# Moving the last 64 keys' value products to another place in an attention visit

## The chip, the core and the metric

The kernel runs on one core of one Trainium2 chip. The metric is the device time of one execution in microseconds (us), smaller being better. Several runs of the kernel are timed and their median is given. One further execution is recorded by the hardware profiler, and every line of a profile in this document comes from such an execution.

## What is computed

The reference normalises the rows of q and k, does attention, lays the heads side by side, and sends the result through a two-layer block whose activation is h - tanh(h):

```python
batch, n_heads, seq, head_dim = (8, 12, 448, 64)
q_n, k_n = (rmsnorm(q, g_q), rmsnorm(k, g_k))
scores = scale * np.matmul(q_n, k_n.transpose(0, 1, 3, 2))
scores = scores - np.max(scores, axis=-1, keepdims=True)
attn = np.exp(scores)
attn = attn / (np.sum(attn, axis=-1, keepdims=True) + 1e-09)
attn_out = np.matmul(attn, v)
x = attn_out.transpose(0, 2, 1, 3).reshape(B * S, H * D)     # 3584 x 768
h = x @ w_in                                                 # w_in 768 x 2048
g = h - np.tanh(h)
return g @ w_out                                             # w_out 2048 x 768
```

All of it is in float32.

## The kernel before

**Steps.** There are 48 steps s, one for each of the 8 batches and 6 pairs of heads. The 448 keys of a head are three blocks of 128 keys and a last block of 64. Scores lie with the keys on the partitions. For a step, `scores(s, c)` (L492) makes one wave of score matmuls: block c = 0, 1 or 2 of both heads, each head into a bank of PSUM of its own, then one exp per head on ScalarE (L512). For c = 3, written `KF`, both halves of the 448 queries are put under one another, so that the wave has 224 columns and not 448. The results are the tiles `p` (blocks 0 and 1), `p_full` (block 2) and `p_last` (the last 64 keys).

**Value products.** `half_values(s, c, av, first)` (L560) gives the value matmuls of block c in two groups: group 0 takes keys 0 to 63 of the block and adds into the bank `av[0]`, group 1 takes keys 64 to 127 and adds into `av[1]`. `last_values(s, av)` (L547) does the last 64 keys: four matmuls of 224 columns into `av[0]`, then four into `av[1]`. All these matmuls use a piece of the TensorE array of 64 rows and 32 columns, so that eight of them fill the array: two row halves by four column groups. A wave in this document is eight matmuls of the program that use the eight pieces; each is float32 and runs as two passes, so the trace shows 16 MATMUL records for a wave, in two rounds of eight.

**Banks.** From step 12 on the scores share three banks in turn (list `sc`, here called A, B and C), and the two `av` banks are fixed. Each `scores` call takes two banks. With the bank order of one visit written as A, B, C: the wave for the last keys takes A and B, block 0 takes C and A, block 1 takes B and C, block 2 takes A and B. A score matmul into a bank waits until the exp of the scores that were there before is done.

**A visit.** From step `FOLDED` = 13 on, the attention of a step is done by `visit(s, av)` (L579), 35 times in all; 34 of these have a next step, and for these the order of matmuls on TensorE is:

1. the scores of the next step's last keys (`scores(s + 1, KF)`, called in `slot`, L1010), into A and B;
2. `wave(*half_values(s, 2, av, True))`: the values of block 2, both groups, which start the sums in `av`;
3. `last_values(s, av)` (L582);
4. for c = 0 and then c = 1: a wave of head 0's scores of step s + 1 with group 1's values, and a wave of group 0's values with head 1's scores. The exp of each head is put on ScalarE's queue after its wave (L588, L590);
5. `divide(s, av)` (L594): ScalarE copies `av[0]` to `xT` (L670), VectorE adds `av[1]` (L671) and multiplies with the reciprocals of the sums of the weights (L675);
6. `scores(s + 1, 2)` (L596): the last wave of scores, heads alternating, into A and B, and its two exps.

**Between visits.** The two-layer block of the previous batch runs as a generator, `mlp()`. Calls of `run(ns)` in `slot` take matmuls from it, worth a given time by a fixed price per matmul, and put them on TensorE between visits (L733: 128 x 128 arrays of weights, 224 moving columns). Its products follow a Strassen-like scheme of seven products per set, in the order 1, 5, 6, 2, 3, 7, 4, with three banks of PSUM (`mm`) in turn; VectorE and ScalarE empty those banks (L787 for product 1, L789 for product 5, L791 for product 6, L795 and L796 for product 7, L799 for product 3, L803 for product 4). Weights are brought in by DMA to a ring of six places, issued from SyncE five products ahead. The order on each engine is written out by hand: each engine takes its instructions in the order in which the program issues them (`manual_schedule`), and semaphores keep the data right. After a visit `slot` issues the loads for later steps and, mixed with calls of `run`, the VectorE work for the sums and norms of the next steps (L537, L538, L458 to L462, L545, L640, L642, L470).

Of the kernel before, what the change touches and what calls it, by code (L numbers as in the profile page):

```python
# [137 lines left out]
def bounded_path(tc, ctx, q, k, v, moe_w_in, moe_w_out, out, g_col, ident, ones, half_ones, neg_half, early):  # L138
# [353 lines left out]
    def scores(s, c, apart=False):  # L492

        rr, kT, qT = turned[s]
        n = S if c < KF else HS
        name, bufs = ("p", 2) if c < 2 else ("p_full", 1) if c < KF else ("p_last", 2)
        if c == 1:
            p = probs[s, 1] = probs[s, 0]
        else:
            p = probs[s, c] = pp.tile([P, 2, 2 if c < 2 else 1, n], F32, name=name, bufs=bufs)  # L500
        tiles = [sc_bank() for _ in range(2)]

        def score(h, i):
            at, first = (i * BL, 0) if c < KF else (i * BL % KR, i * BL // KR * n)
            r = slice(h * D, (h + 1) * D)
            nc.tensor.matmul(  # L506
                tiles[h][i * BL : (i + 1) * BL, :n], lhsT=kT[r, c * P + at : c * P + at + BL],
                rhs=qT[r, first : first + n], start=True, stop=True,
            )

        def exp(h):
            nc.scalar.activation(  # L512
                p[:, h, c if c < 2 else 0, :], tiles[h][:, :n], AF.Exp,
                scale=1.0 if rr is None else rr[:, 0, 2 * c + h : 2 * c + h + 1],
            )

        if apart:
            return [(lambda i, h=h: score(h, i), lambda h=h: exp(h)) for h in range(2)]
        for i in range(P // BL):
            for h in range(2):  # L520
                score(h, i)
        for h in range(2):
            exp(h)
# [23 lines left out]
    def last_values(s, av):  # L547

        v_nat, p = loaded["v", s], probs[s, KF]
        for n in range(2):  # L550
            keys, at = slice(n * KR, (n + 1) * KR), n * HS if s >= FOLDED else 0
            for m in range(2):
                for h in range(2):
                    r = (2 * m + h) * BL
                    nc.tensor.matmul(  # L555
                        av[n][r : r + BL, at : at + HS], lhsT=v_nat[keys, h, KF, m * BL : (m + 1) * BL],
                        rhs=p[keys, h, 0], start=(s < FOLDED), stop=False, skip_group_check=(s >= FOLDED),
                    )

    def half_values(s, c, av, first):  # L560

        v_nat, p = loaded["v", s], full(s)[c]

        def value(g, i):
            m, h = i // 2, i % 2
            keys = slice(g * D, (g + 1) * D)
            nc.tensor.matmul(  # L567
                av[g][i * BL : (i + 1) * BL, :S], lhsT=v_nat[keys, h, c, m * BL : (m + 1) * BL],
                rhs=p[keys, h], start=first, stop=True, skip_group_check=not first,
            )  # L570

        return [lambda i, g=g: value(g, i) for g in range(2)]

    def wave(*work):
        for i in range(P // BL):
            for fn in work:
                fn(i)

    def visit(s, av):  # L579

        wave(*half_values(s, 2, av, True))
        last_values(s, av)  # L582
        for c in range(2):
            v0, v1 = half_values(s, c, av, False)
            if has(s + 1):
                (s0, exp0), (s1, exp1) = scores(s + 1, c, True)
                wave(s0, v1)
                exp0()  # L588
                wave(v0, s1)
                exp1()  # L590
            else:
                wave(v0, v1)
        del loaded["v", s]
        divide(s, av)  # L594
        if has(s + 1):
            scores(s + 1, 2)  # L596
# [68 lines left out]
    def divide(s, av):  # L665
        b, hp = steps[s]
        rs = whole.pop(s)
        x = xT[b, hp] = xp.tile([P, S], F32, name="xT")
        if s >= FOLDED:
            nc.scalar.copy(out=x, in_=av[0][:, :S])  # L670
            nc.vector.tensor_tensor(out=x, in0=x, in1=av[1][:, :S], op=ALU.add)  # L671
        for m in range(2):
            rows = slice(m * D, (m + 1) * D)
            if s >= FOLDED:
                nc.vector.tensor_tensor(out=x[rows], in0=x[rows], in1=rs, op=ALU.mult)  # L675
                continue
            for n in range(2):
                nc.vector.tensor_tensor(
                    out=x[rows, n * HS : (n + 1) * HS], in0=av[n][rows, :HS], in1=rs[n * D : (n + 1) * D],
                    op=ALU.mult,  # L680
                )
        for c in range(NCH):
            del probs[s, c]
        if hp < HC:
            return
        c = hp - HC
        if c == 0:
            tt[b] = tp.tile([P, 3, HC, HS], F32, name="tt", bufs=1)
        eng = nc.vector if b == 0 and c == HC - 1 else nc.gpsimd
        x11, x12, x21, x22 = (xT[b, r][:, n : n + HS] for r in (c, hp) for n in (0, HS))  # L690
        t1, t2, t4 = (tt[b][:, i, c] for i in range(3))
        eng.tensor_tensor(out=t1, in0=x12, in1=x11, op=ALU.subtract)
        eng.tensor_tensor(out=t2, in0=x22, in1=t1, op=ALU.subtract)  # L693
        eng.tensor_tensor(out=x12, in0=x22, in1=x12, op=ALU.subtract)
        eng.tensor_tensor(out=t4, in0=x21, in1=t2, op=ALU.subtract)
# [244 lines left out]
    def has(s):  # L940
        return 0 <= s < NS
# [63 lines left out]
    def slot(s):  # L1005
# [5 lines left out]
        if s < FOLDED:  # L1011
            last_values(s, av)
            totals(s, sc_bank())
            divide(s, values(s, av))
            for c in range(KF):
                scores(s + 1, c)
        else:
            visit(s, av)
# [405 lines left out]
```

## Time and profile before

| | |
|---|---|
| median of 3 runs | 1404.11 us (1401.81 to 1405.44) |
| profiled execution, its own time | 1404.34 us |
| span of the profiled execution (first to last instruction) | 1402.5 us |
| mean granted TensorE clock | 0.992 |
| first and last visit begin (first value matmul of block 2) | 317.76 and 1243.75 us |
| HBM traffic | 214.50 MB read, 33.42 MB written |

Engines are named PE (TensorE's matmuls), PEld (TensorE's weight loads), ACT (ScalarE), DVE (VectorE), POOL (GpSimd) and SP (SyncE). A group's line gives the source line, the engine, the operation, the tiles as out<-in, the shape, the number of instructions, the busy time, the mean duration of one in ns, and the idle time of the engine just ahead of the group with what ended it. A timeline line gives the start in us from the span's start, the duration, and the same names; instructions of one form that follow each other are merged in it, with their number after the x. Matmuls overlap: a MATMUL record of 536 ns in a wave doesn't mean that TensorE is taken for 536 ns, so the distance between the starts of rounds is what counts.

### The profile page before, as it was taken

The numbers are of one execution on the slowest core, as the hardware profiler recorded it, in microseconds if no ns is written. First come the engines' busy times: TensorE is split into PE (matmuls) and PEld (weight loads), VectorE is DVE, ScalarE is ACT, GpSimd is POOL, SyncE is SP. The second block draws the span as 40 slices with busy tenths as digits, with TensorE's granted clock in tenths as the row PEclk, the third lists the DMA queues.
The fourth block names the chain that finished last, engine by engine and source line by source line (L and its number), as shares of the span: only waits on it lengthen the run. The fifth ranks groups of instructions, "written<-read, shape, count | busy, mean of one in ns | idle before, by whom it ended". The sixth has DMA issues, their size and how long they took to land.

```text
span 1402.5 us, 29929 instructions
## 1 busy us (share of the span) xinstructions
PE 1367.2 (97%) x11864; PEld 1135.0 (81%) x11864; DVE 939.3 (67%) x1530; ACT 506.6 (36%) x1153; POOL 556.4 (40%) x348
## 2 busy tenths in 40 slices
PE   6999899999999999999999999999999999999997
PEld 2458664478888888888889988988988998899997
DVE  3999888866756688567867668656885678632311
ACT  5866554234422433233332333224333243301100
POOL 4665555223532246225544246422462254411310
PEclk9999999999999999999999999999999999999999
DMA  7769788864556656666666666666666666366563
GB/s 174 178 187 252 241 253 212 223 188 153 172 150 179 175 167 172 173 152 200 173 153 173 188 159 180 181 158 175 168 165 175 164 183 186 109 188 179 191 193 91
DMA packets 355273, 250.01 MB, mean 178 GB/s; under 512 B 266484, under 2 KB 297396, under 8 KB 355124
## 3 DMA queue, kind: packets, MB, share of 16 engines
q1 hardware_dynamic: 355120, 248.00, 64.7%
q8 instruction: 96, 1.57, 0.5%
q14 instruction: 53, 0.43, 0.1%
q10 hardware_dynamic: 4, 0.00, 0.0%
HBM read 214.50 MB, written 33.42 MB: 177 GB/s over the span
## 4 chain that ended last, share of the span: by engine, by line
PE 87%; DVE 5%; DMA 3%; ACT 2%; SPq 2%; issue 1%; POOL 0%; DVEq 0%; ACTq 0%
PE mm L733 64%; PE sc L506 9%; PE sc L567 6%; PE mm L898 4%; PE sc L555 1%; PE sc L605 1%; DMA w_raw<-in_moe_w_out_dram 1%; DMA gT<-in_moe_w_in_dram 1%; DMA q_nat<-in_q_dram 1%; ACT p L512 1%; SPq L118 1%; PE mm L605 1%; DMA w_f<-w_out 0%; DVE rs L631 0%; DVE w_out L82 0%
## 5 line engine op out<-in xcount | busy, mean ns | idle before, releaser
L733 PE MATMUL mm<-xT,w_f 128*128 128x224 f32 x1392 | 278.2, 354 | 2.3 <-DVE s L789 2.3
L733 PEld LDWEIGHTS mm<-xT,w_f 128*128 128x128 f32 x1392 | 261.3, 190 | 15.9 <-issue 10.2
L733 PEld LDWEIGHTS mm<-gT,w_f 128*128 128x128 f32 x1344 | 252.8, 190 | 13.2 <-issue 13.2
L733 PE MATMUL mm<-gT,w_f 128*128 128x224 f32 x1344 | 263.0, 354 | 0.0
L506 PE MATMUL sc<-qT,kT 64*32 64x448 f32 (+1 forms) x3072 | 219.3, 507 | 11.7 <-ACT p_last L512 7.8
L463 POOL TENSOR_TENSOR rr_mine<-rr_mine,neg_half 128x28 f32<-128x28 f32 x30 | 145.1, 4837 | 205.5 <-DVE rr_mine L462 205.5
L733 PE MATMUL mm<-tt,w_f 128*128 128x224 f32 x1044 | 208.9, 353 | 0.0
L733 PEld LDWEIGHTS mm<-tt,w_f 128*128 128x128 f32 x1044 | 196.6, 190 | 4.8 <-issue 4.4
L733 PE MATMUL mm<-tg,w_f 128*128 128x224 f32 x1008 | 197.7, 352 | 0.0
L770 POOL TENSOR_TENSOR gT<-s,th 128x448 f32<-128x448 f32 x96 | 119.1, 1250 | 189.4 <-ACT th L769 184.5
L733 PEld LDWEIGHTS mm<-tg,w_f 128*128 128x128 f32 x1008 | 190.6, 190 | 0.0
L506 PEld LDWEIGHTS sc<-qT,kT 64*32 64x32 f32 x3072 | 75.3, 106 | 87.7 <-issue 52.9
L671 DVE TENSOR_TENSOR xT<-xT,sc 128x448 f32<-128x448 f32 x35 | 21.7, 621 | 175.5 <-ACT xT L670 146.9
L693 POOL TENSOR_TENSOR tt<-xT,tt 128x224 f32<-128x224 f32 x23 | 31.4, 1367 | 243.6 <-DVE xT L675 222.0
L650 ACT COPY sum_g<-sum 32x14 f32<-32x14 f32 x280 | 56.2, 201 | 183.7 <-DVE sum L642 178.0
L567 PE MATMUL sc<-p,v_nat 64*32 64x448 f32 x1120 | 110.5, 536 | 0.0
L769 ACT ACTIVATE th<-s 128x448 f32<-128x448 f32 x96 | 55.2, 575 | 116.4 <-DVE s L795 57.2
L512 ACT ACTIVATE p<-sc 128x448 f32<-128x448 f32 x120 | 65.3, 544 | 58.0 <-PE sc L506 34.5
L135 POOL TENSOR_TENSOR rr<-rr,neg_half 112x8 f32<-112x8 f32 (+1 forms) x36 | 59.6, 1678 | 61.8 <-DVE rr L134 37.8
L898 PE MATMUL mm<-gT,w_out 128*128 128x448 f32 x192 | 75.5, 548 | 0.2 <-POOL w_out L90 0.2
L898 PEld LDWEIGHTS mm<-gT,w_out 128*128 128x128 f32 x192 | 36.1, 192 | 38.5 <-issue 36.4
L567 PEld LDWEIGHTS sc<-p,v_nat 64*32 64x32 f32 x1120 | 42.0, 107 | 30.6 <-issue 30.6
(151 smaller groups left out, 1853.7 us busy)
## 6 DMA issues: line engine op xcount, KB each, us to landing
w_f<-w_in SPq DMA_DIRECT2D x196, 384.0 KB, 3.3
w_f<-w_out SPq DMA_DIRECT2D x147, 512.0 KB, 4.0
w_raw<-in_moe_w_out_dram SPq DMA_DIRECT2D x16, 768.0 KB, 5.4
out_dram<-th SPq DMA_DIRECT2D x192, 56.0 KB, 1.9
w_in<-w_out SPq DMA_DIRECT2D x21, 384.0 KB, 6.5
qk_nat<-in_q_dram SPq DMA_DIRECT2D x120, 56.0 KB, 2.4
qk_nat<-in_k_dram SPq DMA_DIRECT2D x120, 56.0 KB, 2.4
gT<-in_moe_w_in_dram SPq DMA_DIRECT2D x32, 192.0 KB, 4.2
```

The costliest lines, as they stand in the source:

```text
L135: nc.gpsimd.tensor_tensor(out=r, in0=r, in1=neg_half[:rows], op=ALU.pow)
L463: nc.gpsimd.tensor_tensor(out=mine, in0=mine, in1=neg_half[:, :1].to_broadcast([P, 2 * NJ]), op=ALU.pow)
L506: nc.tensor.matmul(tiles[h][i * BL : (i + 1) * BL, :n], lhsT=kT[r, c * P + at : c * P + at + BL], rhs=qT[r, first : first + n], start=True ...
L512: nc.scalar.activation(p[:, h, c if c < 2 else 0, :], tiles[h][:, :n], AF.Exp, scale=1.0 if rr is None else rr[:, 0, 2 * c + h : 2 * c + h ...
L567: nc.tensor.matmul(av[g][i * BL : (i + 1) * BL, :S], lhsT=v_nat[keys, h, c, m * BL : (m + 1) * BL], rhs=p[keys, h], start=first, stop=True ...
L605: nc.tensor.matmul(av[n][r : r + BL, :HS], lhsT=v_nat[:, h, c, m * BL : (m + 1) * BL], rhs=p[c][:, h, n * HS : (n + 1) * HS], start=False, ...
L650: nc.scalar.copy(out=acc[h * BL : (h + 1) * BL, g], in_=part[g * BL : (g + 1) * BL, h * NJ : (h + 1) * NJ])
L693: eng.tensor_tensor(out=t2, in0=x22, in1=t1, op=ALU.subtract)
L733: nc.tensor.matmul(bank[:, f * HS : (f + 1) * HS], lhsT=w[:, c * width + f, :], rhs=moving[p](c), start=(first and f == 0 and c == 0), sto ...
L769: nc.scalar.activation(th, h, AF.Tanh, bias=0.0, scale=1.0)
L770: eng.tensor_tensor(out=g[:, rows, cols], in0=h, in1=th, op=ALU.subtract)
L898: nc.tensor.matmul(bank[:, :S], lhsT=w_out_row(f, n // HC)[:, n % HC * P : (n % HC + 1) * P], rhs=g[:, f, :], start=(f == 0), stop=(f == C ...
```

## The change

In `visit` the call of `last_values` is taken from its place behind the values of block 2 and put behind the two rounds of the loop over c. It thus stands ahead of `divide` and of the last wave of scores. Nothing else is touched: the matmuls, their operands and their number stay.

```diff
     def visit(s, av):
 
         wave(*half_values(s, 2, av, True))
-        last_values(s, av)
         for c in range(2):
             v0, v1 = half_values(s, c, av, False)
             if has(s + 1):
...
             else:
                 wave(v0, v1)
+        last_values(s, av)
         del loaded["v", s]
         divide(s, av)
         if has(s + 1):
```

On TensorE the eight matmuls of `last_values` move past the 32 matmuls of the loop. On ScalarE the order is the same, and the copy to `xT` (L670), which had no wait for TensorE of its own, has one. On VectorE, GpSimd and SyncE the order of instructions is the same.

## The prediction

> **What bounds the kernel now.** I read the page's busy times first, then its chain of the work that ended last, then the waits, and then the timelines of the visits.
>
> ```profile
> PE 1367.2 (97%) x11864; PEld 1135.0 (81%) x11864; DVE 939.3 (67%) x1530; ACT 506.6 (36%) x1153; POOL 556.4 (40%) x348
> ...
> PE 87%; DVE 5%; DMA 3%; ACT 2%; SPq 2%; issue 1%; POOL 0%; DVEq 0%; ACTq 0%
> ```
>
> TensorE sets the time: it is 97% busy, and 87% of the chain lies on it. But a busy figure hides short stops, because overlapping matmuls cover them. They show in the distances between starts. So I took one visit, the one that begins at 835.87 us, and read the starts on TensorE round by round (a round is eight matmuls, one for each piece of the array). First the rounds around the moved work, with the matmuls of the old place at L555:
>
> ```profile
> 836.24 0.58 PE L567 MATMUL sc<-p_full,v_nat 64*32 64x448 f32 x8
> 836.62 0.58 PE L555 MATMUL sc<-p_last,v_nat 64*32 64x224 f32 x16
> ```
>
> A round of 448 columns takes 0.375 us (836.24 to 836.62). The moved work is two rounds of 224 columns and takes 0.38 us, since block 0's first round starts at 837.00. From there eight rounds follow at 0.375 us each, 837.00 to 840.00, without a stop. Then comes the last wave of scores. Its weight loads, and beside them ScalarE:
>
> ```profile
> 839.63 0.11 PEld L506 LDWEIGHTS sc<-qT,kT 64*32 64x32 f32 x1 [0.22 <-ACT p L512]
> 840.00 0.34 PEld L506 LDWEIGHTS sc<-qT,kT 64*32 64x32 f32 x15 [0.27 <-issue]
> ```
> ```profile
> 838.84 0.55 ACT L512 ACTIVATE p<-sc 128x448 f32<-128x448 f32 x1 [0.22 <-PE sc L506]
> 839.57 0.54 ACT L512 ACTIVATE p<-sc 128x448 f32<-128x448 f32 x1 [0.19 <-PE sc L567]
> 840.34 0.54 ACT L512 ACTIVATE p<-sc 128x448 f32<-128x448 f32 x1 [0.23 <-PE sc L506]
> 840.78 0.53 ACT L670 COPY xT<-sc 128x448 f32<-128x448 f32 x1
> ```
>
> The wave's first matmul (head 0, bank A) starts at 840.00; in a narrower window of the timeline it is alone there, and the other seven start from 840.17 on. The second one (head 1) goes to bank B, whose scores of block 1, head 0, are read by the exp that ends at 839.57 + 0.54 = 840.11. So the whole wave loses 0.17 us to that exp. Afterwards the layer's first matmul (L733) starts at 841.08, which is 0.91 us behind the delayed start: two rounds and the run-out of the small pieces.
>
> The same reading in all 34 visits with a next step gives the same picture: the second matmul starts 0.14 to 0.33 us behind the first, and the sum is 6.3 us (mean 0.185).
>
> **A second place** where TensorE stops is between visits, once per batch, five times in the stretch of visits:
>
> ```profile
> 856.19 1.02 PE L733 MATMUL mm<-xT,w_f 128*128 128x224 f32 x4 [0.46 <-DVE s L789]
> ```
>
> The distance to the matmul before it is 0.63 us too long; the other four (at 530, 693, 1019 and 1182 us) are 0.60, 0.62, 0.55 and 0.72. VectorE comes late to empty a bank of the layer. The chain, read back from there, runs on VectorE alone, without a wait for TensorE, to the end of the visit:
>
> ```profile
> 840.89 0.43 ACT xT L670
> ...
> 841.34 0.63 DVE xT L671
> ...
> 855.52 0.62 DVE s L789
> ```
>
> So an earlier copy to xT moves that late step too.
>
> **What the Trainium skill says.** "TensorEngine Tiling (Array Packing)", Key Properties: tiles run independently, and a change of tiling mode drains the array. The trace agrees: eight matmuls of a round start within 0.05 us, and 841.08 is 0.16 us behind the end of two full rounds from 840.17 (the run-out). The moved matmuls have the tiling of both their old and their new neighbours, so no drain is added. "TensorE: Matmul & The Clock Gate", Part 3, The mechanism: matmuls start in program order, only weight loads are pulled ahead. The trace agrees: one waiting matmul held the six behind it in its round. "PSUM — Partial Sum Buffer", Engine vs sequencer instructions: ScalarE's queue is strictly first in, first out; so the copy's new wait could hold the exps behind it.
>
> **The change, part by part.** Times are within the visit above.
>
> 1. Removed at the old place: 0.375 us of matmuls between block 2's values and block 0's wave. All eight rounds start 0.375 us earlier, and so do the four exps that follow them: they end at 838.24, 839.01, 839.74 and 840.51.
> 2. New exposure of these rounds: head 1's scores of block 0 need bank A, head 0's of block 1 need bank B. The exps of p_last that free A and B begin at 836.21 and end at 836.57 and 836.81. The matmuls come at 837.37 and 838.12, their weight loads one round earlier. Left are 0.8 and 1.3 us to the matmul. In all visits those exps are within 0.1 us of this. Cost nothing; if ScalarE came 0.8 us later, this cover would be gone.
> 3. Added at the new place: two rounds of 224 columns, 0.375 us, from 839.63 to 840.00. TensorE has the same work ahead of the last wave of scores as before, which can again start at 840.00. Each float32 matmul is unchanged.
> 4. The stall: bank B is free at 839.74 plus the 0.06 us that lie between the exp's end and the start seen before, 839.80. The moved work covers this. In the worst visit (0.33 us) the release comes 0.05 us ahead of the wave. Gain 0.17 us here; over 34 visits 6.3 us. The last visit has no scores: nothing.
>    The unknown is how fast weights follow behind the short rounds: before, the eight loads behind L555 took from 836.81 to 836.96 and just fitted. With a wait among them they may end late by 0 to 0.1 us; I take 0, and keep 34 x 0.1 = 3.4 us for the range.
> 5. The new wait on ScalarE: the copy to xT waits for the moved matmuls. The last exp began 0.67 us behind the start of the last matmuls that it reads, of which 0.375 is streaming, so the tail is 0.29 us. The moved matmuls start their second pass at 839.82: 839.87 + 0.19 + 0.29 = 840.35 at the latest. ScalarE itself is free for the copy at 840.78 - 0.375 = 840.41. So the wait is covered by the exp, narrowly. Behind the copy are queued only the two exps of p_full, which need the last wave of scores (done about 841.0 either way).
> 6. VectorE's step L671 begins 0.375 us earlier, TensorE's layer work 0.17 us earlier. The five late emptyings (L789) sit at the end of an unbroken VectorE chain, so they come 0.375 us earlier while TensorE arrives 0.17 us earlier: each stop shrinks by 0.2 us, 1.0 us in all. Bounds: 0 (another step in the chain starts to wait) and 3.1 us (all five go).
> 7. DMA issues, GpSimd and SyncE: nothing is moved in their order. Loads of weights go by TensorE's progress; no matmul of L733 in the visits' stretch is shown waiting for a DMA.
>
> Sum: -6.3 - 1.0 = -7.3 us. Against the profiled execution's own 1404.34 us (span 1402.5 and 1.8 around it) that is 1397.0; it lies 0.2 us above the median of 1404.11, so for a median I say **1396.8 us**. TensorE bounds what follows to the end, with the layers of the last batches, so I expect what is saved in the visits to arrive there whole.
>
> **Rivals.**
>
> A. The forecast: 1396.8, with a spread of 1394.5 (all five stops go as well) to 1399.5.
>
> B. Half the gain: the stall is replaced by late weight loads, 0.1 us per visit, and VectorE's gain doesn't arrive: 1404.1 - 6.3 + 3.4 = 1401.2. For it: loads behind L555 were the slowest of the visit. Against: they fitted.
>
> C. Nothing arrives: TensorE comes 0.17 us earlier and waits for something between visits (a weight tile, a bank): 1404. For it: DMA is busy 60 to 70% in this stretch. Against: the five stops above are all that TensorE shows there, and VectorE gets more time, not less.
>
> D. Slower. The moved work no longer overlaps itself: in its new place the four matmuls on the upper row half and the four on the lower might run one group behind the other, as they are issued (n = 0, then n = 1), behind a round that mixes values and scores. Then it takes 0.75 us, 0.375 more than now, against the 0.185 gained: 34 x 0.19 = 6.5 us, 1410.6. It decides from 0.185 us of lost overlap on. Against: at the old place all 16 records lie in two rounds behind a full round, and the banks of the two halves differ from each other in both places.
>
> That the change doesn't do what it says is excluded: the order of instructions on TensorE shows the eight matmuls in the new place in all 35 visits.
>
> **How the numbers follow.** A 0.78, B 0.08, C 0.08, D 0.06. A change of 0.3% (4.2 us, about what a measurement of this kernel can tell from none) puts the border at 1399.9. A falls below it but for a few hundredths, B just above, C within, D above. Faster 0.79, same 0.15, slower 0.06. The range runs from 1394.5 to 1401.5: it takes in A and B, and leaves out C and D (0.14) and A's edges.
>
> **What would show it.** In the changed profile: block 0's first round 0.75 us behind block 2's values; the moved matmuls 3.75 us behind them in two rounds; the last wave of scores with its eight first-pass matmuls in one round, no wait for ScalarE; L733 at 5.05 us behind the visit's start, not 5.19 to 5.38; L671 about 0.37 us earlier; the five L789 stops at 0.35 to 0.5 us. Wrong would be: moved matmuls that span more than 0.4 us, a stop at banks A or B inside the loop, or new waits of L733.

## The result and the profile after

| | before | changed |
|---|---|---|
| median of 6 runs | 1404.12 us (1401.81 to 1405.44) | 1394.97 us (1393.06 to 1397.86) |
| profiled execution, its own time | 1404.34 us | 1397.86 us |
| span | 1402.5 us | 1396.1 us |
| first visit begins | 317.76 us | 319.21 us |
| from the first visit to the last | 925.99 us | 917.76 us |

The ratio of changed to before is 0.9939 (95% interval 0.9929 to 0.9949; the quotient of the two medians, 0.9935, lies inside it), so the change makes the kernel faster by 0.5 to 0.7%. The profiled execution of the changed kernel is its slowest of the six; its first visit begins 1.45 us later than in the profile of before, in a stretch that the change doesn't touch. The stretch from the first visit to the last (34 visits and what lies between them) is therefore the better yardstick: 8.23 us less.

The page looks as before:

```profile
PE 1360.6 (97%) x11864; PEld 1133.3 (81%) x11864; DVE 940.3 (67%) x1530; ACT 507.9 (36%) x1153; POOL 555.4 (40%) x348
...
PE 87%; DVE 5%; DMA 3%; ACT 2%; SPq 1%; issue 1%; POOL 0%; DVEq 0%; ACTq 0%
```

TensorE has lost 6.6 us of busy time with the same 11864 matmuls: a stop between overlapping matmuls counts as busy here, so what was saved shows there, while the idle time (span less busy time) is 35.3 us before and 35.5 us after. What happened is seen in the visit that answers to the one of the prediction, here from 832.78 us on. First the end of TensorE's visit in the timeline, then the weight loads of the same stretch:

```profile
836.54 0.58 PE L555 MATMUL sc<-p_last,v_nat 64*32 64x224 f32 x16
836.92 0.96 PE L506 MATMUL sc<-qT,kT 64*32 64x448 f32 x16
837.81 0.65 PE L733 MATMUL mm<-xT,w_f 128*128 128x224 f32 x2
```
```profile
836.54 0.15 PEld L555 LDWEIGHTS sc<-p_last,v_nat 64*32 64x32 f32 x8 [0.22 <-issue]
836.73 0.34 PEld L506 LDWEIGHTS sc<-qT,kT 64*32 64x32 f32 x16
837.80 0.30 PEld L733 LDWEIGHTS mm<-xT,w_f 128*128 128x128 f32 x2 [0.73 <-issue]
```

The moved matmuls take 0.38 us in their new place (836.54 to 836.92), as in the old one. The 16 records of the last wave stand in one line now, without the odd first one; the second matmul starts 0.007 us behind the first in all 34 visits. Its loads begin at 836.73, ahead of the matmuls at 836.92. Before, 14 of the 16 loads came together with the late matmuls. L733 starts at 5.03 us from the visit's start (mean of 34), before at 5.24.

ScalarE in the same visit, and then the stop once per batch:

```profile
836.11 0.54 ACT L512 ACTIVATE p<-sc 128x448 f32<-128x448 f32 x1 [0.19 <-PE sc L567]
836.90 0.54 ACT L512 ACTIVATE p<-sc 128x448 f32<-128x448 f32 x1 [0.25 <-PE sc L506]
837.35 0.53 ACT L670 COPY xT<-sc 128x448 f32<-128x448 f32 x1
```
```profile
852.74 1.02 PE L733 MATMUL mm<-xT,w_f 128*128 128x224 f32 x4 [0.29 <-DVE s L789]
```

The exp that frees bank B ends at 836.65, 0.27 us ahead of the last wave; in the tightest of the 34 visits it is 0.12 us. The copy to xT follows the last exp at the same distance as before, both 0.38 us earlier in the visit. The five stops at L789, measured as the excess of the distance between starts over the usual 0.187 us, are 0.40 to 0.46 us, 2.20 us in all, where they were 3.12.

### The profile page after: what moved, and what is told of

It is laid out like the page before. It is cut to its first block, busy times and chain, and to the rows that moved or that the text cites. A ratio compares the mean times of both kernels' runs of the same rounds, so it can differ in the third digit from the quotient of the medians.

```text
span 1396.1 us, 29929 instructions
## 1 busy us (share of the span) xinstructions
PE 1360.6 (97%) x11864; PEld 1133.3 (81%) x11864; DVE 940.3 (67%) x1530; ACT 507.9 (36%) x1153; POOL 555.4 (40%) x348
## 4 chain that ended last, share of the span: by engine, by line
PE 87%; DVE 5%; DMA 3%; ACT 2%; SPq 1%; issue 1%; POOL 0%; DVEq 0%; ACTq 0%
PE mm L733 65%; PE sc L506 9%; PE sc L567 6%; PE mm L898 4%; PE sc L555 1%; DMA q_nat<-in_q_dram 1%; PE sc L605 1%; DMA w_raw<-in_moe_w_out_dram 1%; DMA w_f<-w_out 1%; DMA w_raw<-in_moe_w_in_dram 1%; DVE w_out L82 1%; PE mm L605 1%; DVE w_out L78 0%; DVE rs L631 0%; ACT p L512 0%
## 5 line engine op out<-in xcount | busy, mean ns | idle before, releaser
L733 PE MATMUL mm<-xT,w_f 128*128 128x224 f32 x1392 | 278.2, 354 | 1.4 <-DVE s L789 1.4
L733 PEld LDWEIGHTS mm<-xT,w_f 128*128 128x128 f32 x1392 | 261.3, 190 | 15.0 <-issue 10.2
L733 PEld LDWEIGHTS mm<-gT,w_f 128*128 128x128 f32 x1344 | 252.8, 190 | 12.8 <-issue 12.8
L733 PE MATMUL mm<-gT,w_f 128*128 128x224 f32 x1344 | 263.0, 354 | 0.0
L733 PE MATMUL mm<-tt,w_f 128*128 128x224 f32 x1044 | 208.7, 353 | 0.0
L733 PEld LDWEIGHTS mm<-tt,w_f 128*128 128x128 f32 x1044 | 197.0, 190 | 4.4 <-issue 4.4
L733 PE MATMUL mm<-tg,w_f 128*128 128x224 f32 x1008 | 197.7, 353 | 0.0
L733 PEld LDWEIGHTS mm<-tg,w_f 128*128 128x128 f32 x1008 | 190.6, 190 | 0.0
L506 PEld LDWEIGHTS sc<-qT,kT 64*32 64x32 f32 x3072 | 72.3, 107 | 84.3 <-issue 58.8
L671 DVE TENSOR_TENSOR xT<-xT,sc 128x448 f32<-128x448 f32 x35 | 21.7, 621 | 163.3 <-PE sc L506 118.5
L512 ACT ACTIVATE p<-sc 128x448 f32<-128x448 f32 x120 | 65.2, 543 | 46.8 <-PE sc L506 34.5
```

Of the source, the lines that this page charges most:

```text
L506: nc.tensor.matmul(tiles[h][i * BL : (i + 1) * BL, :n], lhsT=kT[r, c * P + at : c * P + at + BL], rhs=qT[r, first : first + n], start=True ...
L512: nc.scalar.activation(p[:, h, c if c < 2 else 0, :], tiles[h][:, :n], AF.Exp, scale=1.0 if rr is None else rr[:, 0, 2 * c + h : 2 * c + h ...
L733: nc.tensor.matmul(bank[:, f * HS : (f + 1) * HS], lhsT=w[:, c * width + f, :], rhs=moving[p](c), start=(first and f == 0 and c == 0), sto ...
```

## The experiments

Theory 1 is that of the prediction: the last wave of scores waits for the exp that empties bank B, and the moved work covers that wait; beside this, an earlier copy to xT pulls VectorE's chain forward and shrinks the L789 stops. The rivals were that the old place of the matmuls was the costly one, that only VectorE's earlier start counts, or that the order counts whatever waits. All times "from the visit's start" are counted from the first value matmul of block 2; they and the delays are means over 34 visits, and the stops are sums, all from one profile per kernel.

| kernel | L733 | delay of the last wave's second matmul | L671 | L789 stops, sum | all stops of the layer, sum | first to last visit | ratio to before (95%) |
|---|---|---|---|---|---|---|---|
| before | 5.24 | 0.194 | 5.51 | 3.12 | 5.02 | 925.99 | 1 |
| changed | 5.03 | 0.007 | 5.13 | 2.20 | 4.00 | 917.76 | 0.9939 (0.9929 to 0.9949) |
| e1_between_blocks | 5.24 | 0.194 | 5.51 | 3.14 | 5.06 | 926.04 | 0.9997 (0.9989 to 1.0006) |
| e2_inside_block1 | 5.03 | 0.007 | 5.51 | 4.10 | 6.92 | 920.72 | 0.9963 (0.9954 to 0.9973) |
| e3_before_half_exp | 5.06 | 0.024 | 5.51 | 4.08 | 6.84 | 921.59 | 0.9969 (0.9959 to 0.9980) |
| e4_after_exp_twice | 5.45 | 0.405 | 5.39 | 1.36 | 3.14 | 931.31 | 1.0042 (1.0027 to 1.0057) |
| e5_after_half_exp | 5.03 | 0.007 | 5.13 | 2.21 | 3.99 | 917.75 | 0.9939 (0.9925 to 0.9953) |
| e6_copy_first | 5.03 | 0.007 | 4.96 | 1.40 | 3.19 | 916.95 | 0.9939 (0.9926 to 0.9952) |
| e7_fold_later | 5.03 | 0.007 | 5.13 | 0.54 | 0.75 | 914.55 | 0.9921 (0.9909 to 0.9934) |
| e8_both | 5.03 | 0.007 | 4.96 | 0.00 | 0.00 | 913.80 | 0.9909 (0.9896 to 0.9922) |

(A delay of 0.007 us is the usual distance of two matmuls in a round. Stops of up to 0.2 us aren't in the sum for L789. The column behind it takes in every distance of layer matmuls that is longer than the usual one, except those at the beginning of a stretch. The line numbers are those of the kernel before.)

The table closes: in each row the stretch from the first to the last visit differs from that of before by 34 times the shift of L733 plus the change of the sum of all stops, to within 0.06 us (reckoned with unrounded figures). For the changed kernel this is -7.2 and -1.0, against -8.23 measured. So nothing else in that stretch has to be explained.

### e1: out of the old place, but not behind block 1

```diff
             else:
                 wave(v0, v1)
-        last_values(s, av)
+            if c == 0:
+                last_values(s, av)
```

> The values of the last 64 keys stand between block 0's and block 1's waves: away from the old place, but with block 1's four rounds still between them and the last wave of scores. Theory 1 (the last wave waits for the exp that empties bank B, and only work put between that exp's wave and the last wave covers it): nothing changes at the last wave, its second matmul again starts 0.14 to 0.33 us behind the first, time as before, 1404 us within 1. Rival (the old place was the costly one: the short matmuls hold up block 0's waves or their exps): the gain is there without the new place, about 1395 us.

Measured: 1404.12 us, no difference from before. The weight loads of this kernel's timeline, in the visit that begins at 835.65:

```profile
837.53 0.15 PEld L555 LDWEIGHTS sc<-p_last,v_nat 64*32 64x32 f32 x8 [0.22 <-issue]
...
839.79 0.34 PEld L506 LDWEIGHTS sc<-qT,kT 64*32 64x32 f32 x15 [0.27 <-issue]
```

The first loads of the moved matmuls are at 1.9 us from the visit's start and not at 0.4, and block 0's exps come 0.37 us earlier than before. The last wave has the same late 15 loads as before. So leaving the old place, and block 0's earlier exps, bring nothing; the first rival falls.

### e2: behind the wave that fills bank B, ahead of the next one

```diff
                 wave(s0, v1)
                 exp0()
+                if c == 1:
+                    last_values(s, av)
                 wave(v0, s1)
                 exp1()
             else:
                 wave(v0, v1)
-        last_values(s, av)
+                if c == 1:
+                    last_values(s, av)
```

> The values of the last 64 keys stand between the two waves of block 1: behind the wave whose exp frees bank B, but ahead of the wave whose exp the copy to xT follows. Theory 1: the stall at the last wave is covered as in the changed kernel (7.2 us), but ScalarE's copy and VectorE's L671 come at the old distance from the visit's start (5.5 us) while TensorE goes on 0.21 us earlier, so the five L789 stops grow to about 0.84 us each instead of shrinking to 0.44: +1.0 us. Sum -6.2, 1397.9 us. Rival (the gain comes from the earlier copy and VectorE's steps): next to nothing is gained, 1403 us or more. Rival (only the place next to the last wave works): 1404 us.

Measured: 1398.98 us. TensorE's side is as in the changed kernel, 34 x 0.211 = 7.2 us less than before; L671 is where it was before, and the L789 stops grew by 0.98 us. This tells the two parts of theory 1 apart. It refutes the rival that the gain is VectorE's alone, and the rival that the place right ahead of the last wave is needed. The stretch of visits is 5.27 us shorter, and not 6.2. The missing 0.9 us show in what the layer's matmuls waited for (microseconds in all, times; matmuls and weight loads together; this kernel's L792, L794 and L799 are L789, L791 and L796 of the kernel before):

```profile
  DVE s L792: 8.3, 10
  DVE s L794: 1.6, 5
  DVE s L799: 1.4, 5
```

The last line isn't there in the profile of before. Five times, at 18.1 to 18.4 us from the start of the visit one slot ahead of that with the L789 stop, TensorE now comes before VectorE is done with another bank (0.18 us more than before on average, 0.90 in all). Before, VectorE was just in time there: the distances were at most 0.05 us too long.

### e3 and e5: a shorter exp on bank B, before and after

```diff
         def exp(h):
+            m = n if not apart or c != 1 or h else HS
+            if m < n:
+                nc.vector.memset(p[:, h, c, m:], 0.0)
             nc.scalar.activation(
-                p[:, h, c if c < 2 else 0, :], tiles[h][:, :n], AF.Exp,
+                p[:, h, c if c < 2 else 0, :m], tiles[h][:, :m], AF.Exp,
```

The same edit was made to the kernel before (e3) and to the changed kernel (e5).

> The kernel before, with its order of matmuls, but the exp of head 0's scores of block 1 in a visit takes 224 of 448 columns (0.35 us and not 0.54); the other half of these weights is filled with zeros by VectorE, so that part of the attention is left out. Theory 1: bank B comes free 0.19 us earlier, so of the 6.3 us of stalls about 0.7 are left, and a part of the weight loads is ahead again: 5.5 to 6.5 us less; the copy to xT keeps its distance from the visit's start, so the L789 stops grow by 0.15 to 0.2 us each (+0.9): 1398.5 to 1399.5 us. Rival (the order of the matmuls itself is the cause): 1404 us as before.

> The changed kernel with the same shortened exp as in the kernel before (head 0's exp of block 1 takes 224 of 448 columns; the other half of these weights is zero, so a part of the attention is left out). Theory 1 (there is no wait for bank B left): nothing is gained, L733 stays at 5.03 us from the visit's start, the copy and L671 too, since they follow the other head's exp; 1395 us within 1. Rival (a shorter exp is a gain of its own, whatever waits): again about 5 us less, 1390 us.

Measured: 1399.65 us for e3, 1395.70 us for e5. In one visit of e3 and one of e5, the exp for bank B (its L515 is L512 of the kernel before):

```profile
838.24 0.36 ACT L515 ACTIVATE p<-sc 128x224 f32<-128x224 f32 x1 [0.19 <-PE sc L570]
```
```profile
834.78 0.36 ACT L515 ACTIVATE p<-sc 128x224 f32<-128x224 f32 x1 [0.19 <-PE sc L570]
```

In this visit of e3 the exp ends at 838.60, 0.07 us ahead of the last wave, and the wave has no delay. With the order of before, taking 0.19 us from one exp removes 34 x 0.18 = 6.2 us of TensorE's visits; the delay that is left is 0.6 us in all. L671 stays, the L789 stops grow by 0.96, and the late bank of e2 is there as well (0.85), so the stretch is 4.40 us shorter. The time lies 0.15 us beyond the expectation of 1398.5 to 1399.5 us, which left the late bank out. With the changed order the same edit does nothing, neither to the time nor to a figure of the table (the largest difference is 0.01 us). The zeros that VectorE fills in are in both kernels, and in e5 they cost nothing. So it is the wait for this exp that was removed, and nothing of it is left. This is the pair on which I rest the cause.

### e4: the cover used up

```diff
                 exp0()
+                if c == 1:
+                    exp0()
                 wave(v0, s1)
```

(made to the changed kernel)

> The changed kernel, with the exp of head 0's scores of block 1 in a visit issued twice in a row. Theory 1: bank B comes free 0.44 us later, at 4.37 us from the visit's start where the last wave wants it at 4.14: the stall is back with 0.23 us, and 0.03 for weights that are no longer loaded ahead, 34 x 0.26 = 8.8 us; the copy to xT comes 0.1 us later, TensorE 0.26 later, so the L789 stops shrink by 0.16 each (-0.8). Sum +8.0 on 1395.0: 1403 us. Rival (the wait for bank B doesn't matter, the order does): 1395 to 1396 us.

Measured: 1410.08 us, 7 us more than expected. The direction is theory 1's; the expected size was wrong. ScalarE in two narrow windows of one visit's timeline, then the loads for the last wave:

```profile
843.00 0.54 ACT L512 ACTIVATE p<-sc 128x448 f32<-128x448 f32 x1 [0.19 <-PE sc L567]
```
```profile
843.57 0.55 ACT L512 ACTIVATE p<-sc 128x448 f32<-128x448 f32 x1
```
```profile
843.62 0.30 PEld L506 LDWEIGHTS sc<-qT,kT 64*32 64x32 f32 x2
844.17 0.18 PEld L506 LDWEIGHTS sc<-qT,kT 64*32 64x32 f32 x14 [0.26 <-ACT p L512]
```

The second exp begins 0.57 us behind the first, and not 0.44 as the two exps of p_full do. It writes the same part of the same tile, and the trace names the first exp as what it waited for: it begins 0.03 us behind that one's end. So in this visit it ends at 4.45 us from the visit's start and not at 4.31, and the wave's second matmul is 0.37 us late. Over the 34 visits the delay is 0.34 to 0.60 us, 0.405 on average, and not 0.23; the longest are in the first visits, whose exps take 0.63 us and not 0.54. With the weights that are no longer loaded ahead, L733 starts 0.42 us later than in the changed kernel (expected 0.26), 14.4 us in 34 visits; the L789 stops shrink by 0.84, as expected.

### e6 to e8: what is left of the stops at L789

e6 puts the copy ahead of the last exp of block 1:

```diff
                 wave(v0, s1)
-                exp1()
+                if c == 0:
+                    exp1()
...
         divide(s, av)
         if has(s + 1):
+            exp1()
             scores(s + 1, 2)
```

e7 moves two pieces of VectorE's work behind the next stretch of layer matmuls:

```diff
             add_last(s + 1)
+        run(gap / 2)
         if folded:
             fold(s + 1)
-        run(gap / 2)
-        if blocks:
-            scale_blocks(s + 2)
...
         run(gap / 2)
         if blocks:
+            scale_blocks(s + 2)
             turn_blocks(s + 2, 0)
```

e8 has both edits. All three start from the changed kernel.

> The changed kernel with ScalarE's copy to xT ahead of the last exp of block 1. Theory (the five L789 stops follow the start of VectorE's chain, L671): the copy waits for the moved matmuls and starts at about 4.35 us from the visit's start and not at 4.57, L671 at 4.9 and not 5.13, the stops shrink from 0.44 to about 0.25 us each: 1.0 us less, 1394.0 us. Rival (the copy isn't what L671's time comes from, or the late exp holds up TensorE at the next wave): 1395 us or more.

> The changed kernel with two pieces of VectorE work per slot put one stretch of layer matmuls later: the turning and adding up of the sums (L640, L642, 2.2 us) and the scaling of the next q and k (L470, 2.0 us). Theory (the five stops are VectorE's backlog ahead of L789): L789 comes 2.2 us earlier, the stops go, 2.2 us less, 1392.8 us. Rival (the backlog moves to the next bank, L791, or to the sums that the next visit divides by): 1395 us or more, with the stop at another line.

> Both: the copy ahead of the last exp, and the two pieces of VectorE work later. If the five stops are all that VectorE's start decides, the second edit leaves nothing for the first: 1392.8 us, like the second alone. If other matmuls of the layer wait for VectorE too, up to 1 us less than that.

Measured: 1394.98, 1392.54 and 1391.49 us. In e6 the copy starts at 4.40 us, and the last exp of block 1, which began at 4.12 us in the changed kernel, begins behind it at 4.83; L733 stays where it was. L671 comes 0.17 us earlier and the stops shrink by 0.80 us in all, as much as the stretch of visits does (916.95 against 917.76); the time can't show it, since its interval is 0.0026 wide, some 3.6 us.

In e7 all five stops go, and two new ones of 0.27 us come up at L789 in another place, 25.1 us from the start of the visit one slot ahead. With a stop goes what follows it. In the changed kernel the matmul behind each stop starts 0.294 us after the late one and not 0.187, and 2.5 us later comes a stop of 0.14 to 0.17 us at L791, again with the same 0.106 us behind it. So all stops are 4.00 us there and 0.75 in e7, and the stretch is 3.21 us shorter, 1.0 us more than was expected from the five stops alone.

In e8 no stop is left, and the stretch is 0.75 us shorter than in e7: the earlier copy removes the two new ones. The times of e7 and e8 alone don't tell these two apart, since their intervals overlap. Against the changed kernel, e8's interval ends (0.9922) just below where the changed kernel's begins (0.9929).

## Why the prediction was right

The forecast was 1396.8 us; the measured median is 1394.97, 1.8 us lower and inside the range, 0.5 us above its lower edge. That edge stood for a kernel in which all five stops go; they didn't (2.20 us are left), so it is other terms that brought the time down there.

- **Steps 1 to 3** hold: block 0's first round is 0.76 us behind block 2's values, the moved matmuls begin at 3.76 us and take 0.38, the last wave starts at 4.14 us as before, and no round inside the loop waits for ScalarE. Step 2 said that the exps of p_last lie within 0.1 us in all visits; in the first four, whose exps are longer, they end up to 0.2 us later. The cover was wide enough.
- **Step 4** had the right cause (e3 against e5, e1, e2) and was mis-sized. It counted the delays, 6.3 us; L733 moved by 5.240 - 5.028 = 0.212 us, 7.2 us over 34 visits. The difference is what follows the second matmul: L733 came 0.910 us behind it before, in every visit, and comes 0.885 behind it now. The step had the 0.91 before it and booked all that exceeds two rounds, 0.16 us, as run-out; the run-out is 0.135, and 0.025 is the price of weights that weren't loaded ahead. In the delayed wave the loads for 32 columns went out together with the matmuls (14 loads from 840.17 on), and the first-pass records were 560 ns long where they are 536 otherwise. e3 tells the two apart: in six of its visits the wave has no delay, but all its loads save the first begin only with the wave's first matmul, and these waves show 0.910 us and 560 ns too. Where the loads are 0.02 us or more ahead, it is 0.881 to 0.886 us and 536 ns. The late loads feared in this step, up to 0.1 us per visit, didn't come: the loads begin 0.19 us ahead of the wave.
- **Step 5** holds: the copy starts at 4.57 us where 4.54 was expected, and its new wait holds nothing up. e6 shows that ahead of the last exp it could start at 4.40, and that a copy which has to wait does hold the exp behind it in the queue.
- **Step 6** holds in size: L671 came 0.38 us earlier, the stops lost 0.92 us of the 1.0 that were forecast. But it took the five stops for all that TensorE loses between visits. All stops together were 5.02 us and not 3.1, since each of the five drags the stops described under e7 behind it, and e2 and e3 show five more places where VectorE is only just in time. Had the copy not come earlier as well, rival C (new waits between visits) would have been right in part.
- **Sum.** -7.2 and -0.9 make -8.1 of the 8.23 us in the stretch of visits; the last 0.1 us is in the small waits of those five places. The ratio gives 1404.12 x 0.0061 = 8.6 us (7.2 to 10.0). So about 0.9 us of the 1.8 us that the forecast missed is mis-sized terms, step 4's above all, and the rest is inside the scatter of the times.
- **Rivals.** B (late loads) and D (the moved work overlaps less) are refuted by the 0.38 us and the early loads; C (nothing arrives) by the time. e1 and e2 show that in these kernels TensorE's own gain depends on whether the matmuls stand between the wave that fills bank B and the last wave; whether VectorE gains too depends on their standing behind the wave that the copy waits for.

## What to carry to other kernels

When an engine is 97% busy and a wave of overlapping matmuls stands in it, read the distances between starts, not the idle time: 0.19 us per visit were invisible in the busy share. And count what follows a stop, not the stop alone. Between the work that fills a bank for the exp and the work that needs that bank again, put matmuls that don't depend on it; the count of rounds between the two, against the exp's duration, says beforehand whether that pays. And look at what the earlier step starts: here a shift of 0.38 us on ScalarE's copy decided stops about 15 us later. Without that shift (e2) TensorE gained as much in the visits, and the stretch came out 2.96 us longer, of which 1.9 us are in the five stops (4.10 against 2.20).

## What the runs showed that I had not expected

- A delayed wave costs more than its delay: 0.025 us per wave for weights that aren't ahead (0.910 against 0.885 us from the second matmul to L733), whether it is late by 0.03 us (e3) or by 0.34 (e4). Loads that begin 0.02 us ahead of the wave are enough to avoid it (e3).
- A stop of the layer's full-array matmuls costs 0.106 us beyond its length: the matmul behind the late one starts 0.294 us after it and not 0.187, at every stop of more than 0.06 us in the visits' stretch of the ten profiles.
- Two exps that write the same part of a tile began 0.57 us apart (e4), two that write different parts 0.44 us.
- The stretch of visits repeats to 0.05 us between executions of kernels that do the same there (925.99 and 926.04; 917.76 and 917.75), while the start of the first visit moved between 314.8 and 319.2 us in ten profiles. From the last visit's begin to the end it is 158.8 to 159.2 us in all ten. So in the profiled executions what differs beside the visits comes from the stages ahead of them; the executions that weren't profiled don't show it.
